# Block-sparse attention and a token/channel mixer on one core: whole k copies, GpSimd casts, and a list that counts changes of partition quarter

## The chip, the cores and the metric

The kernel runs on one core of a Trainium2 chip. A core has five engines that run their own instruction queues and meet at semaphores: TensorE (PE, matmuls and transposes by matmul, results to PSUM), VectorE (DVE), ScalarE (ACT), GpSimd (POOL) and SyncE (SP, which here only issues DMAs). PSUM is the small accumulation memory of PE; SBUF is the working memory, 128 partitions wide. The metric is device time in microseconds of one launch.

## The reference

Four batches, eight heads, 768 positions, head width 64, all in float32. First a block-sparse causal attention, per batch and head:

```python
k_rep = k.reshape(B, H, n_blocks, block, D).mean(axis=3)      # 12 blocks of 64 keys
gate_scores = np.einsum('bhsd,bhnd->bhsn', q, k_rep)           # blocks of the future: -1e9
top_idx = np.argsort(gate_scores, axis=-1)[..., -3:]           # three blocks, and the own one
scores = where(chosen block and key <= query, q @ k.T / 8, -1e9)
attn_out = softmax(scores) @ v
```

The result, heads side by side (512 wide), is x of a mixer: `h = relu(x.T @ w_tok1) @ w_tok2` over positions (768 to 256 to 768), `u = x + h.T`, then `out = u + relu(u @ w_ch1) @ w_ch2` over channels (512 to 1536 to 512).

## The kernel before, in words

The work is cut into 16 **pairs** of heads, four to a batch (`pair(p)`), and one channel MLP for each batch (`mlp(b)`). A pair goes through these steps:

- Load k and q (SP's queue, L491 or L484) and v (GpSimd's queue, L501). In early pairs the loads are plain and PE turns k and q (L424, 128x128 float32 transposes into PSUM buffers called pm). From pair 6 (q) and 7 (k) the loads are so laid out that DVE's 32x32 transposes (L515, L562) do it.
- Sum k over blocks of 64 (DVE, L528 or L517), spread the sums of the two heads to a block-diagonal tile (GpSimd, `spread`, L510), and copy k, cast to float16, into KA, one head after the other (L320 is the copy of DVE and GpSimd, L318 that of ACT). For early k these are four copies of 64 partitions out of PSUM: two halves of 384 positions, two heads.
- Copy q out of PSUM into QT (128 x 384) and cast it head by head into QA.
- The gate: q times block sums (PE, L604; from pair 6 on in three bfloat16 parts, L619), add the causal bias (L608, L624), the third largest of each row (`MAX8`, L635), compare (L648), clear the own block (L655). The resulting mask is turned (PE, L675, or DVE, L660, from pair 5 on) and copied to twelve extra rows of QA; KA has indicator rows there, so that the score matmul adds a large negative number for blocks not chosen.
- Scores (PE, L696, into two PSUM tiles sc of 1024 columns), exp (ACT, L709, into E), causal mask of the diagonal (GpSimd, L717), times v with a column of ones (PE, L726), divide (DVE, L729, L733) into x.
- Token mixer (PE L744, L758; DVE L761 gives u), then u is turned for the channel MLP: by six PE transposes (L772) and a copy (`uT`), or, for the pairs between the leads `ua` and `ub`, by `turned`: DVE block transposes (L430), a store to a scratch tensor in memory (`turn`, L434) and four loads back (L438).

A batch's MLP is 24 groups of four matmuls (L791), a relu each (ACT L799 or DVE L801), and for each of six rows of 128 positions twelve matmuls (L813), the addition of u (L817) and a store (L821).

Pair 0 (`CUT = 1`) is treated in halves so that it can start early: its k, q, gate and mask come in two parts, and its first score tile needs only the first part.

**What sets the order.** Every step is entered in a `Plan` with the engines it may run on, a cost for each, and a priority: the pair's due time `T(p)` less a lead out of the table `L` (in units of the planner). `Plan.run` is a list scheduler: it simulates the engines, takes for the engine that can start first the ready step of the lowest priority, and picks PSUM and SBUF buffers from rings. The instructions are then written out in that order, engine by engine, each engine's queue running in order. Where PE has nothing to do in the planned order, `fill` (L859) puts in matmuls of zeros to an unused PSUM corner, so that PE's clock does not fall. When the last score tile is done, the four halves of the two sc tiles join the ring of the pm buffers.

Lines that the prediction names: L859 zeros; L424 transposes of k and q; L528 k sums; L510 spread; L604 gate; L675 mask transposes; L696 scores; L772 u transposes; L813 last matmuls; L817 addition of u.

Of the kernel before, what the change touches and what calls it, by code (L numbers as in the profile page):

```python
# [52 lines left out]
L = dict(kd=28.39, qd=28.38, vd=14.55, kt=13.31, kr=28.77, ke=-6.18, qt=21.02, qe=-10.99, q16=13.75, g=20.5, b=21.41,  # L53
         k16=21.8, r=25.24, w1=3.91, w2=-6.05, wc1=11.98, wc2=29.44, tok=8.67, ml=11.38, o0=-3.16, o1=2.55, o2=3.04,
         o3=-0.47, o4=-4.49, o5=0.44, o6=-3.74, o7=-7.56, o8=-2.66, o9=-2.98, o10=-2.08, o11=-1.85, o12=5.6,
         o13=-0.18, o14=1.35, o15=1.65, m0=-2.42, m1=5.05, m2=7.96, m3=-1.6, th=5.48, bd=4.61, cu=-9.01, cs=2.59,
         ua=7.09, ub=19.4, ku=23.14, k0=4.38, k1=1.97, qu=19.48, dq=5.5, dk=6.11, va=-12.77)


FREE = {"PE": 800.0, "ACT": 800.0, "DVE": 2200.0, "POOL": 3800.0, "SP": 800.0}  # L60
# [19 lines left out]
class Op:  # L80
    __slots__ = ("n", "cost", "fn", "pr", "deps", "outs", "bufs", "after", "start", "end", "eng", "wait", "not_before", "port", "base", "open")


class Plan:
# [6 lines left out]
    DMA = 1.15  # L91
# [5 lines left out]
    def op(self, cost, fn, rd=(), wr=(), pr=0.0, not_before=0.0, port=False):  # L97
        o = Op()
        o.n, o.cost, o.fn, o.pr, o.not_before, o.port = len(self.ops), cost, fn, pr, not_before, port
# [23 lines left out]
    def run(self, on_slot_end=None, fill=None):  # L123
# [5 lines left out]
        def slot_for(b):  # L129
            r = b.ring  # L130
            i = min(range(len(r.avail)), key=lambda j: r.avail[j])
            return i, r.avail[i]

        shared = [FREE["POOL"]]

# [3 lines left out]
        def start(o, e):  # L139
            t = max(free[e], o.not_before)  # L140
# [27 lines left out]
        while ready:  # L168
# [6 lines left out]
            for e in free:  # L175
# [3 lines left out]
                for o in ready:  # L179
                    c = o.cost.get(e)  # L180
                    if c is None:
                        continue
                    t = start(o, e)
                    if len(c) > 2 and o.pr > -50.0:
                        t = max(t, dma_free - self.AHEAD)
                        if o.pr > -50.0 and any(x[1:] < (o.pr, o.n) and x[0] <= t for x in loads):
# [19 lines left out]
            if e == "PE" and fill:  # L206
                f = fill(o, free[e], t)
                if f:
                    f.n, f.eng, f.start, f.end = -1, e, free[e], t
                    fillers.append(f)  # L210
            free[e] = t + occ
# [10 lines left out]
            for b in o.bufs:  # L222
                if b.ring is None:
                    continue
                if b.slot is None:
                    b.slot, _ = slot_for(b)
# [49 lines left out]
def kernel(  # L276
# [50 lines left out]
    k16r = sring(3, [128, S], F16, "k16")  # L327
# [30 lines left out]
    pidx, nidx, jidx = np.arange(128), np.arange(NB), np.arange(NJ)  # L358
    mrow = 2 * jidx[None, :, None] + (pidx[:, None, None] >= 64)
    gb1 = -1.0e6 * np.maximum(0, nidx[None, None, :] - mrow)  # L360
    both = np.concatenate([gb1, gb1], axis=2)[:, 1:].astype(np.float32)
# [5 lines left out]
    cst = sb(list(both.shape), FP, "cst")  # L367
    cstc = nc.inline_tensor(both, name="cstc").ap()
    gbias = cst
# [4 lines left out]
    nc.gpsimd.affine_select(out=id32, in_=id32, pattern=[[-1, 128]], compare_op=ALU.not_equal, fill=1.0, base=0, channel_multiplier=1)  # L374
    ks2 = [sb([128, 2, NB], FP, f"ks2_{i}") for i in range(2)]
# [50 lines left out]
    def turned(src, dst, rd, wr, pr, c):  # L426

        tp, d = Buf(k16r), Buf(turnr)
        for i in range(2):
            P.op({"DVE": (487.0, 570.0)}, lambda i=i: nc.vector.transpose(  # L430
                out=tp.t.rearrange("p (f g t) -> p g f t", f=4, t=32)[:, 3 * i:3 * i + 3], in_=src()[:, halves(i)].rearrange("p (g f t) -> p g f t", f=4, t=32)),
                 rd=rd[i], wr=[(tp, i)], pr=pr)
# [16 lines left out]
    def split(src, dst, part, rd, kp, pr):  # L449
# [8 lines left out]
        P.op({"POOL": (850.0, 930.0)}, steps, rd=rd, wr=[(src, 2), (kp, 0), (kp, 1)], pr=pr)  # L458

    def pair(p):  # L460
# [5 lines left out]
        cut = p < CUT  # L466
        straight_q, straight_k = p >= L["dq"], p >= L["dk"]
# [13 lines left out]
        for t, src, e, lead in ((k32, ks_, "SP", "kd"), (q32, qs, "ACT" if p == 0 else "SP", "qd")):  # L481
            if straight_k if t is k32 else straight_q:
                for f in range(4):
                    P.op({e: (570.0, 1600.0, 768 * 13.0 / 16)}, lambda f=f, t=t, src=src, e=e: ENG[e].dma_start(  # L484
                        out=t.t.rearrange("p j x d -> p (j x d)")[32 * f:32 * f + 32].rearrange("t (g i) -> t g i", i=32),
                        in_=src[f // 2, :, 32 * (f % 2):32 * (f % 2) + 32].rearrange("(g t) i -> t g i", t=32)), wr=[(t, f)], pr=t0 - L[lead])
                continue
            for x in range(2):
                for i in range(1 + cut):
                    n = NJ // (1 + cut)  # L490
                    P.op({e: (570.0, 1600.0, 128 * n * 17.6 / 16)}, lambda x=x, t=t, src=src, e=e, i=i, n=n: ENG[e].dma_start(  # L491
                        out=t.t[:, n * i:n * i + n, x, :], in_=src[x, 128 * n * i:128 * n * i + 128 * n].rearrange("(j p) d -> p j d", p=128)),
                        wr=[(t, (x, i) if cut else x)], pr=t0 - L[lead] - (99.0 - 0.2 * i if p == 0 else 0.0))
        if p == 0:
            P.op({"ACT": (1500.0, 1600.0)}, lambda: nc.scalar.activation(out=warm, in_=zero[:, 0:1], func=AF.Exp), pr=-98.0)
            P.op({"ACT": (450.0, 1600.0, 128 * 45 / 16)}, lambda: nc.scalar.dma_start(out=cst, in_=cstc), wr=[(fixed, "cst")], pr=-99.0)
        if p < 3:
            e = "SP" if p else "ACT"
            P.op({e: (450.0, 1600.0, 24 * 135 / 16)}, lambda e=e: ENG[e].dma_start(out=KA.t[64:KR], in_=indc), wr=[(KA, "ind")],
                 pr=t0 - L["qd"] + 0.2 if p else -98.9)  # L500
        P.op({"POOL": (1100.0, 2200.0, 1536 * 17.6 / 16)}, lambda: nc.gpsimd.dma_start(  # L501
            out=VA.t[:, :, :, 0:64], in_=vs.rearrange("x (j p) d -> p x j d", p=128)), wr=[(VA, 0)], pr=t0 - L["vd"])
# [5 lines left out]
        def spread(z):  # L508
            for x in range(2):
                nc.gpsimd.tensor_copy(out=ks2b.t[64 * x:64 * x + 64, x, z], in_=ks3.t[64 * x:64 * x + 64, 0, z])  # L510

        if straight_k:
            KT = Buf(KTr)
            for i in range(2):
                P.op({"DVE": (487.0, 570.0)}, lambda i=i: nc.vector.transpose(  # L515
                    out=KT.t[:, halves(i)], in_=k32.t.rearrange("p j x d -> p (j x d)")[:, halves(i)]), rd=loaded(k32, i), wr=[(KT, i)], pr=t0 - L["ku"])
            P.op({"DVE": (862.0, 945.0)}, lambda: nc.vector.tensor_reduce(  # L517
                out=ks3.t[:, 0], in_=KT.t.rearrange("c (n w) -> c n w", w=64), axis=AX.X, op=ALU.add), rd=[(KT, 0), (KT, 1)], wr=[(ks3, 0), (ks3, 1)], pr=t0 - L["kr"])
            for x in range(2):
                P.op({"POOL": (772.0, 820.0), "ACT": (721.0, 825.0), "DVE": (470.0, 555.0)}, lambda e, x=x: copy(ENG[e], KA.t[0:64, x, :], KT.t[64 * x:64 * x + 64]),  # L520
                     port=True, rd=[(KT, 0), (KT, 1)], wr=[(KA, (x, 0)), (KA, (x, 1))], pr=t0 - L["ke"])
            if not thirds:
                P.op({"POOL": (380.0, 450.0)}, lambda: spread(slice(0, NB)), rd=[(ks3, 0), (ks3, 1)], wr=[(ks2b, 0), (ks2b, 1)], pr=t0 - L["kr"] + 0.1)
        else:
            for i in range(2):
                t = Buf(Rr)
                P.op(pe(slow=3), lambda t=t, i=i: transposed(k32, i, t.t), rd=loaded(k32, i), wr=[(t, 0)], pr=at(i, L["kt"]))
                P.op(dve(HS), lambda t=t, i=i: nc.vector.tensor_reduce(  # L528
                    out=ks3.t[:, 0, 6 * i:6 * i + 6], in_=t.t[:, 0:HS].rearrange("c (n w) -> c n w", w=64),
                    axis=AX.X, op=ALU.add), rd=[(t, 0)], wr=[(ks3, i)], pr=at(i, L["kr"]))  # L530
                if not thirds and (cut or i == 1):
                    z = slice(6 * i, 6 * i + 6) if cut else slice(0, NB)
                    P.op({"POOL": (380.0, 450.0)}, lambda z=z: spread(z), rd=[(ks3, i)] if cut else [(ks3, 0), (ks3, 1)],
                         wr=[(ks2b, i)] if cut else [(ks2b, 0), (ks2b, 1)], pr=at(i, L["kr"]) + 0.1)
                if dual:
                    continue
                for x in range(2):
                    def kev(e, t=t, i=i, x=x):
                        copy(ENG[e], KA.t[0:64, x, halves(i)], t.t[64 * x:64 * x + 64, 0:HS])
                    P.op({**dve(HS), **act(HS)}, kev, rd=[(t, 0)], wr=[(KA, (x, i))], pr=at(i, L["ke"]))  # L540
        if thirds:
            split(ks3, lambda x: kp.t[64 * x:64 * x + 64, :, x, :], lambda h, x: h[64 * x:64 * x + 64], [(ks3, 0), (ks3, 1)], kp, t0 - L["kr"] + 0.1)
        if dual:
            k16 = Buf(k16r, "k16")
            P.op({"POOL": (778.0, 828.0)}, lambda: nc.gpsimd.tensor_copy(
                out=k16.t.rearrange("p (j c) -> p j c", c=128), in_=k32.t.rearrange("p j x d -> p j (x d)")), rd=loaded(k32, 0), wr=[(k16, 0)], pr=t0 - L["k16"])
# [356 lines left out]
```

## Time and profile before

| what | us |
|---|---|
| median of 3 runs | 251.23 (250.78 to 254.77) |
| the profiled execution itself | 251.01 |
| its span, first to last instruction | 249.3 |
| PE busy in the span | 241.2 |
| DVE / ACT / POOL busy | 168.0 / 167.3 / 119.9 |

The page gives busy time by engine, then groups of instructions by source line. The timeline has rows of start, duration, engine, line, operation, tiles (out<-in) and count; in brackets stands the idle time of that engine just before, and what ended it. "PEld" is the weight load of a matmul, "SPq" or "ACTq" a queue that issues DMAs. The answer by stretches gives for each stretch of the span the busy time of each engine, the granted clock of PE and the share of time that the DMA engines are busy (over 1 when packets of several queues are in flight on one engine). The granted clock is 1.00 in all stretches that the prediction uses.

### The profile page before, as it was taken

The page shows a single profiled execution, that of the slowest core. Times are in us where ns is not written, and L with a number is a line of the kernel's source. Part 1 is how long each engine was busy: PE and PEld are TensorE (multiplying, and loading weights), DVE is VectorE, ACT ScalarE, POOL GpSimd, SP SyncE. Part 2 cuts the span into 40 slices and gives each one's busy share as a digit, 9 for nine tenths or more (in the row PEclk, how much of TensorE's full clock was granted, in tenths as well). Part 3 has the DMA queues.
Part 4 walks back from the last instruction along what each step waited for, and adds up shares of the span by engine and source line. Part 5 has one row for each costly group of instructions (what it writes and reads, how often), then busy time and mean ns, then how long its engine had stood idle before and what let it go on. Part 6 is the DMA issues. An engine that isn't in the chain of part 4 may idle for free.

```text
span 249.3 us, 6629 instructions
## 1 busy us (share of the span) xinstructions
PE 241.2 (97%) x2478; PEld 164.8 (66%) x2478; DVE 168.0 (67%) x538; ACT 167.3 (67%) x259; POOL 119.9 (48%) x264
## 2 busy tenths in 40 slices
PE   8899899999999999999999999999999999999994
PEld 8788587887656676667665766567756665554643
DVE  4699988988618889999998899799344522112112
ACT  2487979998768597978997688279744662340620
POOL 5065777568438586787788648453111110000000
PEclk9999999999999999999999999999999999999999
DMA  8999999999829899989899983320221211112112
GB/s 147 218 194 189 207 165 170 170 150 111 141 28 168 152 162 153 130 145 184 146 113 154 190 152 63 106 86 5 67 89 63 74 29 45 42 42 87 43 42 84
DMA packets 119816, 29.31 MB, mean 118 GB/s; under 512 B 113348, under 2 KB 116292, under 8 KB 119784
## 3 DMA queue, kind: packets, MB, share of 16 engines
q1 hardware_dynamic: 89952, 21.32, 42.7%
q0 software_dynamic: 28064, 7.08, 30.2%
q10 hardware_dynamic: 1768, 0.49, 0.9%
q8 instruction: 19, 0.31, 0.6%
q14 instruction: 13, 0.11, 0.2%
HBM read 28.29 MB, written 7.67 MB: 144 GB/s over the span
## 4 chain that ended last, share of the span: by engine, by line
PE 78%; DVE 9%; SPq 4%; issue 3%; POOL 2%; ACT 2%; DMA 2%; DVEq 0%; POOLq 0%
PE pm L791 18%; PE pm L813 17%; PE sc L696 11%; PE pm L726 7%; PE sc L813 4%; SPq L484 4%; PE sc L791 3%; PE pm L744 3%; PE pm L758 3%; PE pm L424 3%; PE pm L604 2%; PE pm L859 2%; DMA q<-in_q_dram 2%; PE pm L619 1%; DVE KA L320 1%
## 5 line engine op out<-in xcount | busy, mean ns | idle before, releaser
L709 ACT ACTIVATE E<-sc 128x1024 f16<-128x1024 f32 (+2 forms) x96 | 84.3, 915 | 22.4 <-PE sc L696 20.9
L717 POOL TENSOR_SCALAR_AFFINE_SELECT E<-E 128x256 f16<-128x256 f16 (+1 forms) x96 | 39.4, 416 | 52.4 <-ACT E L709 50.1
L791 PE MATMUL pm<-uT,wc 128*128 128x384 f16 x332 | 62.0, 326 | 0.0
L813 PE MATMUL pm<-wc,h 128*128 128x512 f16 x240 | 58.2, 379 | 0.0
L791 PEld LDWEIGHTS <-wc 128*128 128x128 f16 x384 | 35.8, 98 | 22.5 <-issue 0.2
L696 PE MATMUL sc<-QA,KA 76*128 76x512 f16 (+3 forms) x264 | 48.4, 301 | 0.3
L813 PEld LDWEIGHTS <-h 128*128 128x128 f16 x312 | 28.4, 98 | 26.4 <-issue 0.7
L799 ACT ACTIVATE h<-pm 128x384 f16<-128x384 f32 x62 | 30.2, 491 | 12.7 <-PE pm L791 12.6
L696 PEld LDWEIGHTS <-KA 76*128 76x128 f16 x264 | 23.5, 98 | 14.3 <-issue 0.8
L817 DVE TENSOR_TENSOR os<-u,pm 128x512 f32<-128x512 f16 x20 | 13.6, 681 | 26.9 <-PE pm L813 25.1
L726 PEld LDWEIGHTS <-E 128*128 128x128 f16 x672 | 25.3, 98 | 4.3 <-issue 0.7
L726 PE MATMUL pm<-VA,E 128*128 128x65 f16 x651 | 26.0, 193 | 0.6 <-DVE QT L320 0.5
L318 ACT CAST QA<-QT 64x768 f16<-64x768 f32 (+1 forms) x23 | 18.4, 801 | 2.5 <-DVE QT L562 2.0
L733 DVE TENSOR_TENSOR x<-pm,rc 128x384 f16<-128x384 f32 x31 | 17.2, 554 | 0.8
L799 ACT ACTIVATE h<-sc 128x384 f16<-128x384 f32 x13 | 6.2, 490 | 16.4 <-DVE os L817 8.7
L761 DVE TENSOR_TENSOR u<-x,pm 128x384 f16<-128x384 f16 x31 | 15.9, 545 | 1.8 <-PE pm L758 1.6
L501 POOL DMA_DIRECT2D VA<-in_v_dram x16 | 16.9, 1056 | 0.4 <-issue 0.2
L801 DVE TENSOR_SCALAR h<-pm 128x384 f16<-128x384 f32 x21 | 11.3, 548 | 6.8 <-PE pm L791 3.7
L729 DVE RECIPROCAL rc<-pm 128x6 f32<-128x6 f32 x31 | 5.8, 187 | 12.5 <-PE pm L726 12.3
L744 PEld LDWEIGHTS <-w 128*128 128x128 f16 x192 | 12.0, 98 | 2.5 <-issue 0.7
L758 PEld LDWEIGHTS <-w 128*128 128x128 f16 x192 | 12.0, 98 | 2.3 <-issue 0.5
L635 DVE MAX8 m<-gm 128x8 f32<-128x12 f32 x160 | 13.0, 156 | 0.3
(85 smaller groups left out, 342.7 us busy)
## 6 DMA issues: line engine op xcount, KB each, us to landing
out_dram<-os SPq DMA_DIRECT2D x23, 256.0 KB, 2.2
k<-in_k_dram SPq DMA_DIRECT2D x40, 96.0 KB, 3.3
q<-in_q_dram SPq DMA_DIRECT2D x40, 96.0 KB, 2.7
VA<-in_v_dram POOLq DMA_DIRECT2D x16, 192.0 KB, 5.8
wc<-in_moe_w_ch_dram POOLq DMA_DIRECT2D x8, 384.0 KB, 5.4
k<-in_k_dram SPq DMA_DIRECT2D x12, 192.0 KB, 5.3
q<-in_q_dram SPq DMA_DIRECT2D x10, 192.0 KB, 5.6
turn<-k SPq DMA_DIRECT2D x7, 192.0 KB, 3.6
```

Of the source, the lines that this page charges most:

```text
L318: e.copy(out=out, in_=in_)
L501: P.op({"POOL": (1100.0, 2200.0, 1536 * 17.6 / 16)}, lambda: nc.gpsimd.dma_start(out=VA.t[:, :, :, 0:64], in_=vs.rearrange("x (j p) d -> p ...
L696: nc.tensor.matmul(out=s.t[:, at:at + 128 * m], lhsT=KA.t[:, x, 128 * kk:128 * kk + 128], rhs=QA.t[:, q0:q0 + m, x, :], start=True, stop=True)
L709: nc.scalar.activation(out=E.t[:, BASE[g_]:BASE[g_ + 1]], in_=s.t[:, 0:WIDTH[g_]], func=AF.Exp, scale=scale)
L717: nc.gpsimd.affine_select(out=o, in_=o, pattern=[[0, len(d)], [1, 128]], compare_op=ALU.is_ge, fill=0.0, base=0, channel_multiplier=-1)
L726: nc.tensor.matmul(out=t[:, jq, :], lhsT=E.t[:, cc:cc + 128], rhs=VA.t[:, x, kk, :], start=(kk == 0), stop=(kk == jq))
L733: P.op(dve(384), lambda a=a, rc=rc, x=x: nc.vector.tensor_tensor(out=xp.t[:, :, 64 * x:64 * x + 64], in0=a.t[:, 0:NJ * 65].rearrange("p (j ...
L744: nc.tensor.matmul(out=m1.t[:, 128 * t:128 * t + 128], lhsT=w1[:, j, 128 * t:128 * t + 128], rhs=xp.t[:, j, :], start=(j == 0), stop=(j == ...
L758: nc.tensor.matmul(out=m.t[:, 128 * j:128 * j + 128], lhsT=w2[:, t, 128 * (j0 + j):128 * (j0 + j) + 128], rhs=h1.t[:, t, :], start=(t == 0 ...
L791: nc.tensor.matmul(out=m.t[:, 0:HS], lhsT=wc1[:, c, 128 * f:128 * f + 128], rhs=uT.t[:, c].rearrange("p (a w) -> p a w", a=4)[:, :, 96 * i ...
L799: nc.scalar.activation(out=o, in_=w, func=AF.Relu)
L813: nc.tensor.matmul(out=m.t[:, 0:wide], lhsT=h2.t[:, f, 128 * jj:128 * jj + 128], rhs=wc2[:, f, w:w + wide], start=(f == 0), stop=(f == NFC ...
```

## The change

1. **k of early pairs.** For pairs 1 to 6 the two PSUM halves of k are each copied whole, 128 partitions by 384, to a float16 tile k16 in SBUF (ACT or DVE). From there GpSimd or DVE copies each head (64 x 768) into KA. Pair 0 keeps its copies out of PSUM, now behind the k sum.
2. **q casts** of pairs 1 to 5 are given to GpSimd alone (lead `qp`); the `spread` of block sums may go to DVE.
3. **The list** counts changes of partition quarter: each step says from which memory and quarter it reads and to which it writes (`io`), and a step whose quarter differs from the one before on its engine starts later by `HELD`. It also prefers, among free PSUM buffers, pm over halves of sc; costs of DMAs are set lower (`DMA` 1.1, v's packets 16.0), and a load waits for others that are due within 900 ns.
4. **The first gate and the loads.** k and q of pair 0 are split over SP's and ACT's queues head by head (before: k on SP, q on ACT). The causal bias is made by GpSimd in place of a load. Early pairs have a table of leads of their own (`e...`), and all leads have new values; `ua` 7.09 becomes 3.23 (pairs 4 to 14 are `turned`, before 8 to 14), `bd` 4.61 becomes 5.16 (from pair 6 on DVE turns the mask).
5. One store of the last batch is cut in three, so that the number of DMAs is a multiple of eight.

As issued, the program has 103 matmuls of zeros in place of 95, 30 u transposes in place of 54, 30 mask transposes in place of 25; 12 whole k copies, 12 casts from k16 (7 on GpSimd, 5 on DVE); q's casts 15 on GpSimd (before 8), 13 on ACT (before 21) and 2 on DVE (before 1); 12 of 14 spread copies on DVE.

```diff
-FREE = {"PE": 800.0, "ACT": 800.0, "DVE": 2200.0, "POOL": 3800.0, "SP": 800.0}
+LEADS = ("kd", "qd", "vd", "kt", "kr", "ke", "qt", "qe", "q16", "g", "b", "tok")
+FREE = {"PE": 800.0, "ACT": 800.0, "DVE": 2200.0, "POOL": 3300.0, "SP": 800.0}
...
-    DMA = 1.15
+    DMA = 1.1
+    HELD = {"DVE": 115.0, "ACT": 130.0, "POOL": 85.0}
...
+            twin = lambda j: r.avail[j ^ 1] if r.name == "R" and j >= 4 else 0.0
+            return min(range(len(r.avail)), key=lambda j: (max(r.avail[j], t - self.SYNC), twin(j), r.avail[j]))
...
+        def held(o, e):
+            if not o.io or e not in places or len(o.cost[e]) > 2:
+                return 0.0
+            src, dst = o.io[0].split(">")
+            at = places[e]
+            marks = ["r" + src[i:i + 2] for i in range(0, len(src), 2)] + ["w" + dst]
+            return self.HELD[e] if any(at.get(m[:2], m[2]) != m[2] for m in marks) else 0.0
...
         def start(o, e):
-            t = max(free[e], o.not_before)
+            t = max(free[e] + held(o, e), o.not_before)
...
-    cst = sb(list(both.shape), FP, "cst")
-    cstc = nc.inline_tensor(both, name="cstc").ap()
+    gbias = sb([128, NJ - 1, 2 * NB], FP, "gbias")
+    nc.gpsimd.memset(gbias, 0.0)
+    nc.gpsimd.affine_select(out=o, in_=o, pattern=[[128, NJ - 1], [0, 2], [-64, NB]], compare_op=ALU.is_ge, fill=-1.0e6, base=128, channel_multiplier=1)
...
+        lead = {n: L["e" + n if p < PPB else n] for n in LEADS}
...
             for x in range(2):
+                e = "ACT" if p == 0 and x else "SP"
...
+                if not cut:
+                    def kout(e, t=t, i=i):
+                        copy(ENG[e], k16.t[:, halves(i)], t.t[:, 0:HS])
+                    P.op({**dve(HS), **act(HS)}, kout, rd=[(t, 0)], wr=[(k16, i)], io="P0>S0", pr=at(i, lead["ke"]))
                     continue
...
+        if not straight_k and not dual and not cut:
+            for x in range(2):
+                P.op({"POOL": (772.0, 820.0), "DVE": (300.0, 380.0)}, lambda e, x=x: copy(ENG[e], KA.t[0:64, x, :], k16.t[64 * x:64 * x + 64]),
+                     port=True, rd=[(k16, 0), (k16, 1)], wr=[(KA, (x, 0)), (KA, (x, 1))], io=f"S{2 * x}>S0", pr=t0 - lead["ke"] + 0.1)
...
-                P.op({"POOL": (772.0, 820.0), "ACT": (721.0, 825.0), "DVE": (470.0, 555.0)} if not cut else {"DVE": (300.0, 380.0), "ACT": (410.0, 510.0)},
-                     q16, port=True, ...
+                P.op({"DVE": (300.0, 380.0), "ACT": (410.0, 510.0)} if cut else {"POOL": (772.0, 820.0)} if p < L["qp"] else
+                     {"POOL": (772.0, 820.0), "ACT": (721.0, 825.0), "DVE": (470.0, 555.0)}, q16, port=True, ...
```

More of the change, by code (lines that the diff above doesn't have):

```diff
@@ L80 @@
 class Op:
-    __slots__ = ("n", "cost", "fn", "pr", "deps", "outs", "bufs", "after", "start", "end", "eng", "wait", "not_before", "port", "base", "open")
+    __slots__ = ("n", "cost", "fn", "pr", "deps", "outs", "bufs", "after", "start", "end", "eng", "wait", "not_before", "port", "base", "open", "io")
 class Plan:
@@ L185, in run @@
                         t = max(t, dma_free - self.AHEAD)
-                        if o.pr > -50.0 and any(x[1:] < (o.pr, o.n) and x[0] <= t for x in loads):
+                        if o.pr > -50.0 and any(x[1:] < (o.pr, o.n) and x[0] <= t + 900.0 for x in loads):
                             continue
@@ L783, in mlp @@
         n = 0
+        even = -sum(1 for o in P.ops for e, x in o.cost.items() if len(x) > 2 and e != "POOL") % 8 if b == B - 1 else 0
         for i in range(2):
```

163 lines of the change are left out of this document (88 added, 75 removed).

## The prediction

> **What bounds the kernel now.** First the page's head and the busy time by stretch: where is TensorE (PE) not full?
>
> ```profile
> span 249.3 us, 6629 instructions
> ...
> PE 241.2 (97%) x2478; PEld 164.8 (66%) x2478; DVE 168.0 (67%) x538; ACT 167.3 (67%) x259; POOL 119.9 (48%) x264
> ```
>
> ```profile
> core 0: us, PE busy (x) PEld busy (x) DVE busy (x) ACT busy (x) POOL busy (x), PEclk, DMA share, GB/s
> 0.00:13.57 13.57, 11.04 (x111) 10.18 (x112) 7.75 (x31) 5.36 (x11) 4.94 (x26) 1.00 1.13 184
> 13.57:20.00 6.43, 5.81 (x57) 5.02 (x57) 6.13 (x22) 5.57 (x9) 3.73 (x9) 1.00 1.42 196
> 20.00:30.00 10.00, 9.45 (x110) 7.37 (x110) 9.55 (x31) 8.52 (x12) 6.69 (x18) 1.00 1.17 199
> 30.00:40.00 10.00, 9.65 (x131) 7.87 (x128) 8.41 (x39) 8.68 (x12) 6.66 (x17) 1.00 1.57 159
> 40.00:100.00 60.00, 59.85 (x733) 43.54 (x732) 47.49 (x152) 49.22 (x77) 40.39 (x84) 1.00 1.07 140
> 100.00:150.00 50.00, 49.92 (x536) 32.79 (x534) 46.83 (x148) 42.10 (x63) 37.76 (x72) 1.00 1.03 152
> ```
>
> From 40 us on PE is full, so what leaves PE there is worth its whole time and what any other engine saves is worth nothing by itself. Before 40 us PE idles 2.53 us up to its first scores at 13.57 and 0.62 + 0.55 + 0.35 = 1.52 us behind them; much of the rest of the front is L859, matmuls of zeros that compute nothing. So the timeline of the front is read next.
>
> ```profile
> 0.82 2.13 ACTq L491 DMA_DIRECT2D q<-in_q_dram  x4
> ...
> 0.82 4.01 SPq L491 DMA_DIRECT2D k<-in_k_dram  x6
> ...
> 1.07 3.33 PEld L859 LDWEIGHTS <-zero 128*128 128x128 f16 x34 [1.07 <-DVE zero L372]
> ...
> 1.09 0.29 POOL L374 TENSOR_SCALAR_AFFINE_SELECT id<-id 128x128 f32<-128x128 f32 x1
> ...
> 4.45 0.85 PE L424 MATMUL pm<-id,k 128*128 128x128 f32 x3
> ...
> 5.09 0.85 PE L424 MATMUL pm<-id,q 128*128 128x128 f32 x3
> 5.34 0.56 DVE L528 TENSOR_REDUCE ks<-pm 128x6 f32<-128x384 f32 x1 [2.54 <-PE pm L424]
> ...
> 5.81 1.11 DVE L320 CAST KA<-pm 64x384 f16<-64x384 f32 x2
> ...
> 5.98 0.48 ACT L318 COPY QT<-pm 128x384 f32<-128x384 f32 x1 [1.50 <-PE pm L424]
> ...
> 6.60 0.78 PE L604 MATMUL pm<-ks,QT 128*128 128x12 f32 x4
> 6.96 0.55 DVE L320 CAST QA<-QT 64x384 f16<-64x384 f32 x1
> ...
> 7.82 1.15 PEld L859 LDWEIGHTS <-zero 128*128 128x128 f16 x20
> ...
> 9.19 0.54 DVE L528 TENSOR_REDUCE ks<-pm 128x6 f32<-128x384 f32 x1
> ...
> 10.24 0.85 PE L604 MATMUL pm<-ks,QT 128*128 128x24 f32 x6 [1.11 <-POOL ks L510]
> ...
> 11.40 0.82 DVE L635 MAX8 m<-gm 128x8 f32<-128x12 f32 x10
> ...
> 12.14 0.30 DVE L648 TENSOR_TENSOR bn<-pm,m 128x72 f16<-128x72 f32 x2
> ...
> 12.43 0.19 DVE L655 MEMSET bn<- 64x6 f16 x2
> ...
> 13.06 0.96 ACT L318 COPY QA<-pm 12x384 f16<-12x384 f16 x2
> ...
> 13.57 0.93 PE L696 MATMUL sc<-QA,KA 76*128 76x256 f16 x9
> ...
> 15.14 1.02 DVE L320 COPY QT<-pm 128x384 f32<-128x384 f32 x2
> ...
> 16.20 0.55 DVE L320 CAST QA<-QT 64x768 f16<-64x768 f32 x1
> 16.30 1.13 POOL L320 CAST QA<-QT 64x768 f16<-64x768 f32 x1 [0.42 <-DVE QT L320]
> ```
>
> The chain to the first scores: k transposed, k summed (DVE), sums spread (POOL), gate (PE), top three and mask (DVE), mask transposed (PE) and copied (ACT). Its worst hole is before the second gate at 10.24: the second k sum starts only at 9.19, behind DVE's two k casts and the q copies.
>
> **Term 1, the front: -2.9 us.** The order of the changed kernel walked with the durations above:
> - 28 zeros in place of 34, at 3.33/34 = 0.098 us: PE is free at 1.07 + 2.7 = 3.8. The first k halves now head both load queues.
>
> ```profile
> DMA to landing us min/median/max: 2.6/3.6/6.2
> ```
>
> - At the least of this row (k, first 8 us) they land at 0.82 + 2.6 = 3.4, so the zeros still decide. k transposes 3.8; four zeros; q transposes 4.8.
> - Sum 0.89 behind its transposes (5.34 against 4.45): 4.7 to 5.3. The spread is DVE's now: no such DVE row; between the memset pair (0.19) and a pair of half-height casts (1.11), nearest the memset by size, I take 0.3: 5.6. q's copy 0.89 behind its transposes, on DVE: 5.7 to 6.25. First gate about 6.4 (was 6.60).
> - DVE goes on with q's cast (to 6.8), the second k sum (to 7.35, was 9.73), the first half of the gate scores (0.15), the spread (to 7.8), four MAX8 (0.33), compare and memset: half of the mask at about 8.5 (was 12.62).
> - ACT has k casts, QA cast, k cast, then the second q copy, to 8.35: second gate 8.4 (was 10.24), to 9.25.
> - Two mask transposes and the next pair's six k transposes (1.2 us) on PE, while ACT finishes two casts and copies the half mask (under 0.96): first scores at 10.5.
>
> That is 3.1 earlier, less 0.2 for three mask transposes that move behind. Bounds: -1.5 (the whole mask is needed by the second scores anyway and lands on the same DVE) to -4.0 (spread at 0.19, nothing queued at ACT).
>
> **Term 2, new zeros behind the first scores: +2.5 us.** The order has 60 zeros after the first scores, 17 before the change: the list sees holes there (16, 10 and 11 in a row between the scores of pairs 1 to 2). 43 x 1.15/20 = 2.5. Bounds +1.0 (they stand where PE would have idled, 1.52 now) and +3.2 (each of some six more holes is longer than its zeros by two pitches). The front's gain thus partly runs into ACT and DVE, which cannot follow at that speed.
>
> **Term 3, waits behind the first scores: -1.0 us.**
>
> ```profile
> PEld pm L424 <- DVE KA L320: 1.7, 3, 0.8
> ```
>
> The transposes of k and q wait for PSUM buffers that DVE's half-height k casts hold. Now a buffer is read by the sum and one whole copy (0.51 each in the pair at 15.14) instead of the sum and two casts (0.555 each). Also the list now charges VectorE, ScalarE and GpSimd for a change of partition quarter; the two pairs of rows, 1.02 and 1.11, show that such a charge exists, so waits that the order did not foresee should shrink. Of 1.52 I take 1.0; bounds 0 and -1.5.
>
> **Term 4, PE work: -1.06 us.** Lead "ua" goes from 7.09 to 3.23: u of pairs 4 to 7 is turned by DMA, 24 transposes fewer; "bd" keeps pair 5's mask on PE, five more.
>
> ```profile
> 44.74 0.67 PE pm L744 x12
> ```
>
> 128 columns take 0.67/12 = 0.056: 19 fewer are -1.06, all where PE is full.
>
> **Term 5, the end: -0.4 us.**
>
> ```profile
> 245.63 0.49 PE L813 MATMUL sc<-wc,h 128*128 128x128 f16 x6 [0.38 <-DVE os L817]
> ```
>
> The last two output sums lie in halves of one sc tile; the second waits until DVE has read the first. Now they lie in two pm tiles, and the late MLP uses no sc half at all: four buffers in place of eight. Its cover: a relu takes 0.49, a group of PE 0.65.
>
> ```profile
> L799 ACT ACTIVATE h<-pm 128x384 f16<-128x384 f32 x62 | 30.2, 491 | 12.7 <-PE pm L791 12.6
> ```
>
> A fourth-last buffer has three groups' time, 1.95, to be read. If that cover went, each group would wait some tenths.
>
> **Costed at nothing:** the bias made by GpSimd (two instructions more, at most 0.29 each by the row at 1.09; the loads hide them, and without that cover the first V load starts 0.6 later, long before E needs V); KA's indicator rows, now ACT's fifth load issue in place of its sixth, as the constant's is gone; one out store of the last batch cut in three, two more issues for SP while PE computes the last batch.
>
> Sum: -2.9 + 2.5 - 1.0 - 1.06 - 0.4 = -2.9. The profiled run took 251.01 us (span 249.3 and 1.7 around it; median of the runs 251.23): **248.1 us**, own range 246.2 to 250.5.
>
> **Rivals.**
>
> *GpSimd is the next late one.* It takes on 7 k casts and 7 q casts net, most before 60 us.
>
> ```profile
> L320 POOL CAST KA<-KT 64x768 f16<-64x768 f32 x10 | 8.2, 818 | 2.6 <-DVE bn L648 1.3 <-DVE KT L515 1.1
> ...
> L320 POOL COPY QA<-bnt 12x384 f16<-12x384 f16 x16 | 8.0, 499 | 4.9 <-DVE bnt L660 4.4
> ```
>
> At 0.82 (fp16 input is not shown; half the columns take 0.50) that is 11.5 us. The masks of E queue behind them. The cast at 16.30 took 1.13 while DVE's cast at 16.20 ran: 0.31 more. If all 14 meet DVE so and PE waits each time: 14 x 0.31 = 4.3, 252.4 us. For it: DVE is 9.55 of 10 busy from 20 to 30. Against: POOL has 3.3 us free in each 10. It decides once POOL is past 9.5 of 10 there. [...]
>
> *Slower: the loads.*
>
> ```profile
> q1 hardware_dynamic: 89952, 21.32, 42.7%
> ```
>
> ```profile
> SPq L434 <- DVE k L430: 17.5, 4, 5.8
> ```
>
> The DMA share is above 1 from 40 to 150 us. A packet of q1 takes 0.427 x 249.3 x 16/89952 = 0.019 us on one engine; a turned u is 1024 packets, 1.2 us of all 16; four more are 4.8 us, between 60 and 100. SP also issues in order: pair 8's k and q now stand behind turn stores, which wait for DVE up to 5.8 us. PE would stand at the gates of pairs 8 to 12, which it meets in order. If the loads lag by the whole 4.8 and the front's gain is eaten there: 251.0 - 1.06 - 0.4 + 4.8 = 254.3 us. Against: the gates of pairs 9 to 15 stand later in PE's order than before (pair 15's now behind pair 14's scores). It decides when a gate's k lands after PE has reached it.
>
> *More than forecast.* Front -4.0, zeros +1.0 (they cover what were waits), waits -1.5, then -1.06 and -0.5: -6.1, 244.9 us. For it: the list now knows costs that the trace shows.
>
> **How the numbers follow.** Forecast 0.46, GpSimd 0.20 (250 to 253), loads 0.12 (252.8 to 257), more 0.22 (243.5 to 246.2). The range 244.6 to 252.8 leaves out the loads and the lowest of the last. Two per cent, about what a measurement of this kernel tells from no change, is 5.0 us: below 246.2 lies the last case and an edge of the first, 0.24; above 256.3 a part of the loads, 0.05; within 0.71.
>
> **What would show it.** Term 1: first scores near 10.5 us, second gate near 8.4. Term 2: zeros of 0.5 us and more between 15 and 35 us, with ACT at 9 tenths. Term 3: no wait of k transposes on DVE casts. Term 4: 30 u transposes. Term 5: no wait of the last sums on DVE. GpSimd: casts over 1 us, E masks late and PE waiting on them. Loads: PE idle at the gate line between 85 and 140 us. I am wrong if PE is no longer full behind 40 us.

## The result, and the profile after

The changed kernel took 247.43 us (median of 6 runs, 246.32 to 251.24); the kernel before, on the same chip, 251.14 (median of 6). The ratio is 0.985, 95% interval 0.981 to 0.988: 3.7 us less by the medians, forecast 3.1 (251.2 to 248.1). The profiled execution is the lowest of the six, 246.32 with a span of 244.6, so 4.7 below the profiled one of before. Ratios and their intervals, here and below, leave out runs that lie over 1.5% above the kernel's lowest; medians keep them.

The page's head, and the answer by stretches:

```profile
span 244.6 us, 6642 instructions
...
PE 238.1 (97%) x2467; PEld 162.9 (67%) x2467; DVE 170.4 (70%) x546; ACT 160.6 (66%) x251; POOL 128.2 (52%) x263
```

```profile
0.00:10.61 10.61, 8.01 (x74) 7.23 (x75) 5.74 (x30) 5.50 (x11) 3.75 (x21) 1.00 1.14 175
10.61:20.00 9.39, 8.41 (x110) 7.14 (x108) 8.13 (x30) 7.98 (x13) 7.35 (x15) 1.00 1.33 207
20.00:30.00 10.00, 10.00 (x121) 8.75 (x117) 8.66 (x34) 7.71 (x11) 7.58 (x13) 1.00 1.34 211
30.00:40.00 10.00, 9.91 (x142) 7.85 (x141) 8.33 (x38) 7.68 (x11) 8.63 (x19) 1.00 1.95 168
40.00:100.00 60.00, 59.99 (x720) 43.18 (x719) 51.79 (x153) 44.41 (x72) 42.08 (x85) 1.00 1.01 148
100.00:150.00 50.00, 50.00 (x541) 33.16 (x540) 46.05 (x142) 40.93 (x61) 38.29 (x75) 1.00 1.19 167
```

But for 0.1 us PE is busy from 20 us on, where it was from 40. Busy is not the same as useful, though: 39 of the matmuls between 20 and 30 us are zeros, some 2 us of time, and between 20 and 40 us 216 matmuls that compute start, where it was 220. The lead is made before: by 20 us 128 of them have started, where it was 88. ACT went down from 167.3 to 160.6, GpSimd up from 119.9 to 128.2. The timeline of the front, with the rows that answer to those of before:

```profile
3.85 0.85 PE L446 MATMUL pm<-id,k 128*128 128x128 f32 x3
...
4.74 0.56 DVE L553 TENSOR_REDUCE ks<-pm 128x6 f32<-128x384 f32 x1 [2.94 <-PE pm L446]
...
5.41 0.34 DVE L534 COPY ks<-ks 64x6 f32<-64x6 f32 x2
5.78 0.56 DVE L344 COPY QT<-pm 128x384 f32<-128x384 f32 x1
...
6.49 0.58 PE L639 MATMUL pm<-ks,QT 128*128 128x12 f32 x4 [0.15 <-DVE QT L344]
...
6.85 0.54 DVE L553 TENSOR_REDUCE ks<-pm 128x6 f32<-128x384 f32 x1
...
8.53 0.82 PE L639 MATMUL pm<-ks,QT 128*128 128x24 f32 x6 [0.71 <-DVE bn L683]
...
10.61 0.83 PE L731 MATMUL sc<-QA,KA 76*128 76x256 f16 x10
...
22.82 1.00 PE L899 MATMUL pm<-zero 128*128 128x120 f16 x16
```

The whole list of PE's waits:

```profile
PE pm L899 <- DVE zero L391: 1.1, 1, 1.1
PE pm L639 <- DVE bn L683: 0.7, 1, 0.7
PE pm L446 <- DMA k<-in_k_dram: 0.7, 2, 0.3
PE pm L446 <- DMA q<-in_q_dram: 0.6, 1, 0.6
PE sc L731 <- DVE QA L344: 0.3, 1, 0.3
PE pm L639 <- DVE QT L344: 0.2, 1, 0.2
```

All of them lie before 15 us. Three are for loads (0.7 for k, 0.6 for q, all but the first for the pairs behind pair 0), a wait that PE's list of before does not have. The waits of the k transposes on DVE's casts and that of the last sums on DVE are gone.

### The profile page after: what moved, and what is told of

It is laid out like the page before. It is cut to its first block, busy times and chain, and to the rows that moved or that the text cites. A ratio compares the mean times of both kernels' runs of the same rounds, so it can differ in the third digit from the quotient of the medians.

```text
span 244.6 us, 6642 instructions
## 1 busy us (share of the span) xinstructions
PE 238.1 (97%) x2467; PEld 162.9 (67%) x2467; DVE 170.4 (70%) x546; ACT 160.6 (66%) x251; POOL 128.2 (52%) x263
## 4 chain that ended last, share of the span: by engine, by line
PE 91%; DMA 3%; DVE 3%; issue 0%; SPq 0%; POOL 0%; POOLq 0%
PE pm L827 26%; PE pm L849 25%; PE sc L731 14%; PE pm L761 9%; PE pm L779 4%; PE pm L793 4%; DMA k<-in_k_dram 3%; PE pm L639 2%; PE pm L654 2%; PE pm L446 2%; PE pm L710 1%; PE pm L899 1%; DVE ks L553 1%; DVE ks L534 1%; PE pm L807 1%; DVE m L670 1%
## 5 line engine op out<-in xcount | busy, mean ns | idle before, releaser
L827 PE MATMUL pm<-uT,wc 128*128 128x384 f16 x384 | 69.9, 326 | 0.0
L849 PE MATMUL pm<-wc,h 128*128 128x512 f16 (+2 forms) x312 | 68.8, 363 | 0.0
L835 ACT ACTIVATE h<-pm 128x384 f16<-128x384 f32 x71 | 34.5, 491 | 28.2 <-PE pm L827 28.0
L853 DVE TENSOR_TENSOR os<-u,pm 128x512 f32<-128x512 f16 (+2 forms) x26 | 16.6, 640 | 33.9 <-PE pm L849 33.2
L796 DVE TENSOR_TENSOR u<-x,pm 128x384 f16<-128x384 f16 x32 | 16.5, 542 | 4.7 <-PE pm L793 4.7
L837 DVE TENSOR_SCALAR h<-pm 128x384 f16<-128x384 f32 x25 | 13.8, 554 | 8.5 <-PE pm L827 7.5
L768 DVE TENSOR_TENSOR x<-pm,rc 128x384 f16<-128x384 f32 x32 | 17.8, 555 | 0.9
L793 PE MATMUL pm<-h,w 128*128 128x128 f16 x192 | 13.8, 219 | 0.0
L342 ACT COPY QA<-bnt 12x384 f16<-12x384 f16 x20 | 10.2, 508 | 5.3 <-DVE bnt L695 4.9
L779 PE MATMUL pm<-x,w 128*128 128x128 f16 x192 | 13.3, 219 | 0.0
```

The source lines that it names most:

```text
L768: P.op(dve(384), lambda a=a, rc=rc, x=x: nc.vector.tensor_tensor(out=xp.t[:, :, 64 * x:64 * x + 64], in0=a.t[:, 0:NJ * 65].rearrange("p (j ...
L779: nc.tensor.matmul(out=m1.t[:, 128 * t:128 * t + 128], lhsT=w1[:, j, 128 * t:128 * t + 128], rhs=xp.t[:, j, :], start=(j == 0), stop=(j == ...
L793: nc.tensor.matmul(out=m.t[:, 128 * j:128 * j + 128], lhsT=w2[:, t, 128 * (j0 + j):128 * (j0 + j) + 128], rhs=h1.t[:, t, :], start=(t == 0 ...
L827: nc.tensor.matmul(out=m.t[:, 0:HS], lhsT=wc1[:, c, 128 * f:128 * f + 128], rhs=uT.t[:, c].rearrange("p (a w) -> p a w", a=4)[:, :, 96 * i ...
L835: nc.scalar.activation(out=o, in_=w, func=AF.Relu)
L849: nc.tensor.matmul(out=m.t[:, 0:wide], lhsT=h2.t[:, f, 128 * jj:128 * jj + 128], rhs=wc2[:, f, w:w + wide], start=(f == 0), stop=(f == NFC ...
```

## The experiments

Each kernel was timed against the kernel before. In the table the last column has those runs in which PE's granted clock stood at 0.998 or more over the whole run; why it is needed is told at zeros_gone. Below, these runs are compared with each other, and medians with medians. zeros_gone, k_in_place and closer_zeros keep the changed kernel's order of work; by the traces turn_undone keeps PE's up to 62 us and slots_undone up to 200. The others are planned anew from the front on, and what that alone can cost is seen at jitter_a.

| kernel | median us | ratio to before, 95% | runs at full clock, us |
|---|---|---|---|
| changed kernel | 247.43 | 0.985 (0.981 to 0.988) | 246.32, 246.54 |
| front_only | 254.09 | 1.011 (1.010 to 1.013) | 253.28, 253.30 |
| turn_undone | 248.28 | 0.988 (0.986 to 0.990) | 247.28 |
| slots_undone | 247.10 | 0.984 (0.981 to 0.986) | 245.90 |
| zeros_gone | 250.60 | 0.984 (0.982 to 0.986), from 3 of its 12 runs | 246.17, 247.60 |
| old_leads | 250.61 | 1.001 (0.998 to 1.003) | 249.68 to 250.48 |
| k_undone | 251.12 | 1.001 (0.998 to 1.004) | 249.15, 249.63 |
| q_undone | 250.76 | 0.997 (0.994 to 1.001) | 249.00 to 249.81 |
| quarters_undone | 251.93 | 1.002 (0.999 to 1.004) | 249.65 |
| jitter_a | 255.47 | 1.020 (1.016 to 1.023) | none |
| jitter_b | 250.78 | 0.998 (0.995 to 1.001) | 248.82, 248.91 |
| k_in_place | 249.30 | 0.995 (0.992 to 0.998) | 248.76 to 249.21 |
| closer_zeros | 246.81 | 0.984 (0.981 to 0.986) | 246.13 to 246.98 |

**front_only: the front alone, on the kernel before.**

```diff
-        for t, src, e, lead in ((k32, ks_, "SP", "kd"), (q32, qs, "ACT" if p == 0 else "SP", "qd")):
+        for t, src, e, lead in ((k32, ks_, "SP", "kd"), (q32, qs, "SP", "qd")):
             for x in range(2):
+                e = "ACT" if p == 0 and x else "SP"
...
-                nc.gpsimd.tensor_copy(out=ks2b.t[64 * x:64 * x + 64, x, z], in_=ks3.t[64 * x:64 * x + 64, 0, z])
+                ENG[e].tensor_copy(out=ks2b.t[64 * x:64 * x + 64, x, z], in_=ks3.t[64 * x:64 * x + 64, 0, z])
```

(with the bias by GpSimd and the new leads of pair 0)

> The kernel before with the front alone changed: pair 0's loads split over SP and ACT by head, the bias made by GpSimd, its spread open to DVE, its leads those of the change. Theory (the early start carries through, because PE is full behind it): first scores about 3 us earlier than the 13.57 of before, and of that at least half reaches the end, 248.5 to 249.8 us. Rival (the front runs into ScalarE and VectorE, which set the pace from 14 to 40 us, and the gain is only real together with the relief of those two): first scores early too, but PE idle and zeros between 14 and 40 us grow by as much, and the time stays within 0.7 us of before.

The first scores start at 11.34, 2.2 earlier than before, and the kernel is 3.2 us slower than before by the medians. By stretches:

```profile
20.00:30.00 10.00, 9.65 (x94) 7.41 (x91) 9.26 (x31) 9.19 (x15) 4.84 (x12) 1.00 1.16 207
30.00:40.00 10.00, 9.97 (x140) 8.63 (x139) 8.29 (x38) 8.58 (x13) 6.19 (x17) 1.00 1.75 178
40.00:50.00 10.00, 8.80 (x120) 6.89 (x117) 7.32 (x28) 8.65 (x13) 6.32 (x13) 1.00 1.34 162
```

DVE and ACT are over 9 of 10 busy from 20 to 30 while GpSimd is at 4.84; PE idles 1.2 between 40 and 50. Behind the first scores stand 58 matmuls of zeros where 17 stood before: 41 more, at 0.052 us each 2.1 us, as much as the early start gained, while PE's idle time from the first scores to 60 us stays as it was (1.64 and 1.67). So far the rival is right: the early start runs into zeros, and the two engines that empty PSUM are the ones that are nearly full. Why the kernel is 3 us slower on top of that isn't shown; it has a new order too, and the profiled run has one stretch at half clock (10.7 to 14.1 us).

**turn_undone, slots_undone: `ua` back to 7.09; the old choice of a PSUM buffer.**

```diff
-          ua=3.23, ...
+          ua=7.09, ...
```

```diff
-            return min(range(len(r.avail)), key=lambda j: (max(r.avail[j], t - self.SYNC), twin(j), r.avail[j]))
+            return min(range(len(r.avail)), key=lambda j: r.avail[j])
```

> The changed kernel with lead ua back at 7.09: u of pairs 4 to 7 is turned by PE again, 24 transposes of 0.056 us. Theory (PE is full behind 40 us): 1.3 us slower than the changed kernel, 247.7 us for a profiled run against 246.3. Rival (the four stores and sixteen loads more cost DMA time that PE waits for at the gates): no slower, or up to 1 us faster, and less PE idle between 85 and 120 us.

> The changed kernel with PSUM buffers picked as before, the longest free first, halves of sc included. Theory (a wait on the other half of one sc tile cost time at the end): PE waits again behind 200 us, 0.4 to 1.2 us in all, and the run is that much slower than the changed kernel. Rival (four pm buffers instead of eight cost as much in waits on the relus as they save): no difference beyond 0.3 us.

turn_undone has 54 u transposes again and takes 0.85 us more by the medians, 0.74 to 0.96 at full clock (one run): the theory's sign, at two thirds of its 1.3. slots_undone is no slower (its rival is right), and in its trace too PE has no hole over 0.1 us behind 200 us: that rule alone isn't what removed the wait of the last sums. turn_undone's price comes near to one in a held order, but it is no surer than the half microsecond by which slots_undone lies below the changed kernel at full clock.

**zeros_gone: no zeros behind a planned 10 us.**

```diff
-        if mlp_on or n < 2:
+        if mlp_on or n < 2 or a > 10000.0:
```

> The changed kernel without the 60 matmuls of zeros that stand behind its first scores; everything else is in the same order, and the result is the same. Theory (the zeros stand where PE would idle, as holes of the order): no faster than 0.4 us, and the idle time of PE between 11 and 57 us grows by about 2 to 3 us, as much as the zeros took. Rival (the zeros are themselves a cost, run before work that is ready): 1.5 to 3 us faster. A third way: slower by 0.5 us or more, if matmuls run slower after idle time.

The third way came, by the clock of PE: two runs of twelve are at full clock, ten take 249.60 to 252.96. Stretches of 3.4 us of a profiled run (the column before the last two is the granted clock):

```profile
4.70:8.10 3.40, 2.77 (x29) 2.20 (x27) 3.03 (x12) 2.02 (x5) 0.00 (x0) 1.00 1.56 185
8.10:11.50 3.40, 2.26 (x22) 2.09 (x23) 2.46 (x17) 2.31 (x6) 0.00 (x0) 1.00 1.35 225
11.50:15.00 3.50, 3.31 (x18) 1.95 (x17) 3.36 (x8) 2.42 (x5) 2.26 (x6) 0.51 1.21 214
15.00:18.40 3.40, 3.40 (x18) 3.17 (x17) 0.33 (x2) 1.83 (x2) 2.97 (x5) 0.50 0.85 184
18.40:21.80 3.40, 3.40 (x32) 2.71 (x30) 2.52 (x17) 2.52 (x4) 1.24 (x3) 0.50 1.21 177
21.80:25.00 3.20, 3.20 (x50) 2.94 (x48) 2.48 (x6) 1.13 (x3) 2.61 (x4) 1.00 0.91 195
```

PE idles 1.14 of the 3.40 us up to 11.5, no hole longer than 0.71; then the clock stands at half for three stretches. At full clock the two runs, 246.17 and 247.60, stand beside 246.32 and 246.54: no gain is shown, and a loss of up to 1 us isn't excluded. That fits zeros that stand where PE would idle. What they buy is the clock: without them it falls in ten of twelve runs, for three or four stretches by the mean clock (0.972 to 0.979); with them in four of six.

The changed kernel itself has this in smaller measure. Its six runs by mean clock: 246.32 (1.000), 246.54 (0.999), 247.31 and 247.54 (0.993), 248.09 (0.986), 251.24 (0.973). Each 0.007 is one stretch of 3.4 us at half clock (3.4/2/245), so there were one, one, two and four, and costs 0.8 to 1.2 us.

**old_leads: the whole code of the change with the leads of before.**

```diff
-L = dict(kd=28.39, qd=24.29, vd=11.04, ... etok=17.72)
+L = dict(kd=28.39, qd=28.38, vd=14.55, ... (the values of before, for early pairs too), qp=5.5)
```

> The changed kernel with the due times of before: every lead in the table, early pairs too, has the value it had (so u of pairs 4 to 7 is turned by PE again and pair 5's mask by DVE); whole k copies, GpSimd casts, counted quarters, the new loads and the bias stay. Theory (the parts themselves carry the gain, the table only fits them): 247.5 to 249.5 us. Rival (an early start and freed engines are worth little until the due times of the steps behind them are moved to use it; the front alone was 3.2 us slower than before): 250.5 us or more, with PE idle and zeros between 14 and 50 us above the 6.8 us of the changed kernel.

By the medians no gain is left (250.6), at full clock some 0.5 us (249.68 to 250.48, where before took 250.4 to 251.7 beside it): the rival is right in the main. The reverse, a table fitted anew to the code of before, wasn't tried; so how much of the gain the search for a better table would give without the parts stays open.

**k_undone, q_undone, quarters_undone: one part undone, all leads new.**

```diff
-                if not cut:
+                if False:
                     def kout(e, t=t, i=i):
```

```diff
-          ... dq=5.5, qp=5.5, ...
+          ... dq=5.5, qp=0.5, ...
```

```diff
-    HELD = {"DVE": 115.0, "ACT": 130.0, "POOL": 85.0}
+    HELD = {"DVE": 0.0, "ACT": 0.0, "POOL": 0.0}
```

> The changed kernel, but k of pairs 1 to 6 copied again head by head out of PSUM, four copies to a pair, on VectorE or ScalarE. Theory (PSUM buffers held by these copies made PE wait, and VectorE and ScalarE set the pace of the front): 0.8 to 2.5 us slower than the changed kernel, with waits of the k and q transposes on copies back in the trace. [...]

> The changed kernel, but q's casts of pairs 1 to 5 may go to any of GpSimd, ScalarE and VectorE again. Theory (ScalarE's exps set the pace from 14 to 40 us and casts stand in their way): 0.3 to 1.5 us slower. Rival (GpSimd late, casts meeting VectorE's copies): as fast or up to 1 us faster, since the list may pick the freest engine.

> The changed kernel with the list's charges for a change of partition quarter set to zero. Theory (a list that knows these waits puts its zeros and steps where the chip has them): 0.5 to 2 us slower, with more PE idle and fewer zeros (92 for 103) between 10 and 40 us. Rival (an order like any other): within 0.4 us.

Each alone loses nearly the whole gain, 2.5 to 3.5 us at full clock and 3.3 to 4.5 by the medians: three parts with all of it each cannot be a sum. Either each is needed, or any disturbance of the planned order costs this much. Two tests tell these apart.

**jitter_a, jitter_b: nothing undone, every lead moved at random by up to 0.3 us (but those that switch a pair from one way to another, such as ua).**

```diff
-L = dict(kd=28.39, qd=24.29, vd=11.04, kt=13.4, ke=-12.17, ...)
+L = dict(kd=28.17, qd=24.5, vd=11.2, kt=13.25, ke=-12.2, ...)
```

> The changed kernel with every lead of the table moved at random by up to 0.3 us (a pair takes 16.5), and nothing else: all parts of the change are kept. Each part undone alone took the time back to 250.6 to 251.9, nearly the whole gain. Theory 'the table fits one order': it is the particular order that the table gives that is worth 3 to 4 us, and any disturbance of the list loses it; then this kernel too takes 249.5 to 251.5 us, and what a part undone alone costs is mostly that. Rival 'the parts carry it': the order is not so sensitive, this kernel stays within 1.2 us of the changed one (246.3 to 248.6), and k's whole copies, q's casts and the quarter charge are each worth about 3 us in this order.

> The same with another draw of the random moves. Theory 'the table fits one order': 249.5 to 251.5 us. Rival 'the parts carry it': 246.3 to 248.6. If the two draws differ by more than 1.5 us from each other, the order itself is worth that much, and the cost of a part undone alone cannot be read as the price of the part.

With every part in place the time is 255.5 and 250.8; jitter_b at full clock 248.82 and 248.91, 2.3 to 2.6 above the changed kernel, and jitter_a has no run at full clock. By stretches, jitter_a and then jitter_b:

```profile
10.00:20.00 10.00, 9.91 (x54) 8.50 (x55) 4.57 (x23) 5.37 (x9) 5.23 (x10) 0.50 1.29 211
...
100.00:150.00 50.00, 48.84 (x523) 31.86 (x520) 45.86 (x140) 38.69 (x59) 38.86 (x77) 1.00 1.08 163
```

```profile
10.00:20.00 10.00, 9.87 (x85) 8.48 (x86) 5.73 (x27) 7.02 (x12) 5.89 (x11) 0.69 1.12 193
...
100.00:150.00 50.00, 48.43 (x507) 31.32 (x504) 43.62 (x127) 39.88 (x57) 36.84 (x71) 1.00 1.20 165
```

Both lose in two places: the granted clock is 0.50 and 0.69 between 10 and 20 us, and PE idles again after 100 us (1.2 and 1.6), where the changed kernel is full. The theory that the table fits one order holds; so the price of an undone part cannot be read from the three kernels above, nor from old_leads and front_only. The fall of the clock isn't the leads' doing alone, as the changed kernel has it in four of six runs; the 2.3 to 2.6 us at full clock are the measure.

**k_in_place: k's copies undone, the order held.**

```diff
-                        copy(ENG[e], k16.t[:, halves(i)], t.t[:, 0:HS])
+                        for x in range(2):
+                            copy(ENG[e], KA.t[0:64, x, halves(i)], t.t[64 * x:64 * x + 64, 0:HS])
...
-lambda e, x=x: copy(ENG[e], KA.t[0:64, x, :], k16.t[64 * x:64 * x + 64]),
+lambda e, x=x: None,
```

> The changed kernel with its order of work held: the planner plans whole copies of k as in the changed kernel, but at the place of each whole copy (pairs 1 to 6, twelve copies of 128x384) two half-height casts straight into KA are made by the same engine, and the later copies into KA (which GpSimd mostly did) are not made at all. PE, ACT and DVE keep the order and the places of the changed kernel; only the engines' times differ: about 0.6 us more in each of twelve places on DVE or ACT (1.11 a pair for 0.51 one), 7 us between 10 and 85 us, and some 8 us less on GpSimd. When k's copies were undone with a new plan the time was 251.1, 3.7 above the changed kernel. Theory 'the order is what was lost': here the loss is at most 1.2 us, 247.0 to 248.6. Rival 'the whole copy itself carries the gain': the PSUM buffers are held 0.6 us longer each time, PE waits behind most of the twelve, 249.5 to 252.

The median falls between the two forecasts. Six of its twelve runs are at full clock, 248.76 to 249.21, 2.2 to 2.9 above the changed kernel. Its timeline near 22 us, and then that of the changed kernel at the same place:

```profile
22.34 1.95 ACT L342 CAST KA<-pm 64x384 f16<-64x384 f32 x4 [2.00 <-PE pm L446]
...
25.39 0.43 PE L732 MATMUL sc<-QA,KA 76*128 76x512 f16 x2 [1.04 <-ACT E L745]
```

```profile
21.82 0.86 ACT L342 CAST k<-pm 128x384 f16<-128x384 f32 x2 [2.17 <-PE pm L446]
...
22.59 2.54 ACT L744 ACTIVATE E<-sc 128x1024 f16<-128x1024 f32 x3
```

The casts hold ACT 1.95 in place of 0.86, the exps start later, and the scores wait 1.04 for a PSUM tile. PE is busy 8.39 and 8.77 of 10 between 10 and 30 us, against 9.02 and 10.00. With the order held, k's whole copies are worth about 2.5 us in this order, which was fitted to them. Sixteen of the 24 casts are ACT's here and the longest new wait names its exps, so the place is at least in part ACT's. That is no step back to the kernel before, which had 20 of its 28 half-height casts (pair 0's included) on DVE. How much q's casts and the quarter charge carry in a held order wasn't tried.

**closer_zeros: zeros priced by what they take.**

```diff
-        n = int((b - max(a, at + 60.0)) / (54.0 if a > 16000.0 else 104.0) - 1.0)
-        if mlp_on or n < 2:
+        n = int((b - max(a, at + 60.0)) / (54.0 if a > 7000.0 else 104.0) - 1.0)
+        if mlp_on or n < 1:
```

> The changed kernel with the planner's zeros priced 54 ns in place of 104 from the planned 7 us on, and single zeros allowed: holes between 7 and 16 us are filled about twice as densely (14, 1, 8, 5, 6 zeros where 7, 0, 3, 2, 2 stood; 124 in all for 121). Theory: the dips of the granted clock that cost the changed kernel 0.8 to 1 us each come from holes of TensorE between 5 and 14 us; with them filled most runs show a clock of 1.0, and the median falls from 247.4 to 246.3 (0.3 to 1.1 less than the changed kernel). Rival 'zeros only get in the way': each new zero lies before work that was ready, the front grows by up to 17 x 0.055 = 0.9 us and the clock dips as often: 247.4 to 248.3.

Median 246.81, and all six runs lie between 246.13 and 247.65: one of six has a half-clock stretch where the changed kernel had four. At full clock it gains nothing. Its interval overlaps that of the changed kernel, so a gain of 0.6 in the median isn't proven, and six runs are few to call the missing tail shown.

## Why the prediction was right

Forecast -2.9 against the profiled run, measured -4.7 (its clock at 1.00 throughout, and the lowest of its six runs) and -3.7 by the medians. The main case came, with every sign right, and the front came nearly step by step. The sizes are less sure than the total: by the busy time of the views the five terms add up to -3.2 and 0.3 lies behind the last matmul; the other 1.2 lies in time that the records call busy, where the ends of matmuls are modelled, and no term named it. That the median comes so near is in part luck: the profiled runs, both at full clock, gained 1.8 more than forecast, and the clock took back 1.0 of it in the median.

- **Term 1, the front.** First scores forecast at 10.5, seen at 10.61 (-2.96; the term's -2.9 has 0.2 off for mask transposes that move behind). Step by step, forecast and seen: k transposes 3.8 / 3.85; q 4.8 / 4.76; first gate 6.4 / 6.49; second k sum 6.8 / 6.85; second gate 8.4 / 8.53. The spread on DVE, taken at 0.3 between bounds of 0.19 and 1.11, took 0.34.
- **Term 2, zeros.** +2.5 forecast, +2.2 in the trace: behind the first scores stand 17 zeros before and 60 after, at 0.052 each (the row at 22.82: 16 in 1.00, the last of them 0.22 long), 0.9 and 3.1. As a row of the sum it stands; as the price of zeros it was wrong in kind: zeros_gone gains nothing at full clock without them. Terms 2 and 3 are better read as one: PE's time behind the first scores that computes nothing, zeros and idle time to 200 us, rose from 0.9 + 1.75 to 3.1 + 1.08, by 1.5, as the two terms together said. So about half of what the front gained was lost behind it.
- **Term 3, waits.** -1.0 forecast; by the busy time of the views PE's idle time from the first scores to 200 us falls from 1.75 to 1.08, -0.7. Counted between the starts of matmuls, beyond the pitch of their shape, it falls by 1.0 to 2.0, an estimate that depends on the pitch taken. The transposes' wait on DVE's casts is gone as forecast. Whether the gain came from DVE, where the step looked for it, isn't settled; k_in_place shows that ACT's share in the copies counts too.
- **Term 4, PE work.** -1.06 forecast, as 24 u transposes fewer (-1.34) and five mask transposes more (+0.28). turn_undone puts the 24 back and costs 0.85, in an order that is the same up to 62 us: the sign is shown, the size only roughly. The mask transposes were priced too low, 0.056 each: five of them take 0.47 in the row at 24.81 of the changed kernel. 30 u transposes, as forecast:

```profile
L807 PE MATMUL pm<-id,u 128*128 128x128 f16 x30 | 2.5, 219 | 0.0
```

- **Term 5, the end.** -0.4 forecast, -0.7 measured in idle time behind 200 us. By stretches, before and then after, each nearly to PE's last matmul:

```profile
200.00:245.60 45.60, 44.95 (x296) 25.35 (x295) 9.10 (x16) 15.92 (x34) 1.22 (x3) 1.00 0.13 49
```

```profile
200.00:241.30 41.30, 41.30 (x273) 23.36 (x270) 7.73 (x14) 13.85 (x29) 0.00 (x0) 1.00 0.14 50
```

  After idles nothing there; before had, beside the hole of the last sums (0.38), one of 0.30 at 204.9 that the forecast did not name:

```profile
205.20 0.83 PE L744 MATMUL sc<-x,w 128*128 128x128 f16 x12 [0.30 <-DVE x L733]
```

  Which edit closed them isn't settled: neither the slot rule nor the leads alone, since slots_undone and old_leads lack them too.
- **GpSimd as the next late one** didn't come. It is 7.58 and 8.63 of 10 busy from 20 to 40 us, short of the 9.5 that the forecast named, and no wait in PE's list names it. Its meetings with DVE are there, in the timeline of the changed kernel:

```profile
11.79 0.82 POOL L344 COPY KA<-k 64x768 f16<-64x768 f16 x1 [0.19 <-DVE k L344]
...
12.14 1.44 DVE L534 COPY ks<-ks 64x12 f32<-64x12 f32 x2
...
13.50 0.72 DVE L344 COPY QA<-pm 12x384 f16<-12x384 f16 x2
...
13.89 0.98 PE L731 MATMUL sc<-QA,KA 76*128 76x384 f16 x7 [0.32 <-DVE QA L344]
...
14.05 0.81 POOL L344 CAST QA<-QT 64x768 f16<-64x768 f32 x1 [0.49 <-ACT QT L342]
14.25 0.82 DVE L344 COPY KA<-k 64x768 f16<-64x768 f16 x1
...
18.10 0.48 DVE L534 COPY ks<-ks 64x12 f32<-64x12 f32 x2
...
24.48 0.35 DVE L344 COPY KA<-k 64x768 f16<-64x768 f16 x1
```

  A KA copy of DVE takes 0.82 where it starts behind a cast of GpSimd (at 14.25, the cast at 14.05) and 0.35 where it starts first (at 24.48); the two copies of a spread take 1.44 where GpSimd's KA copy and masks of E run, and 0.48 where only the first of them meets the end of a KA copy. The copy at 14.25 ends at 15.07, 0.21 behind GpSimd's cast; what holds it isn't shown. The loss falls mostly on DVE: its five KA copies take 0.35 to 0.87, GpSimd's seven KA copies and 15 q casts 0.81 to 0.84. Once PE pays: the copies of the mask start only behind the spread of 1.44, and the scores at 13.89 wait 0.32 for them.
- **Slower, the loads** didn't come: the stores of turned u wait up to 10.1 us for DVE, 9.6 where the wait is for the turning transposes (forecast: up to 5.8),

```profile
SPq L456 <- DVE k L452: 17.8, 5, 9.6
SPq L456 <- DVE rc L764: 14.1, 2, 10.1
```

  and still PE has no wait at a gate behind 15 us.
- **More than forecast** came near in the runs at full clock (246.3 to 246.5; that case began at 246.2), by the time that no term named and by term 5. The prediction had no case in which PE's clock falls below 1.00; that it falls in four of six runs brings the median back by 1.0.

## What to carry to other kernels

Where an order of work has been fitted, undo a part with the order held before you price it: here a random 0.3 us on the leads cost nearly as much as any part, 2.3 to 2.6 us at full clock. Fit the table to the old code anew as well; that wasn't done here, so the gain belongs to the parts and the new table together. An earlier start pays only if what it runs into can follow: alone it turned into zeros (41 more, 2.1 us, in front_only). Count zeros apart from work when PE looks full. And where the clock falls in some runs of one program, compare runs of equal clock before medians.

## What the runs showed of the hardware

The clock of PE fell to half for 3.4 us, or two, three or four times that, in nine of the fourteen traces, always once and between 9 and 12 us while work was under way. It lasted 3.4 us in front_only, turn_undone, slots_undone (0.50 from 10.3 to 13.7 us) and old_leads, and by the mean clock of the stretches about 6.8 in q_undone and jitter_b, 10.2 in zeros_gone and 13.6 in quarters_undone and jitter_a. No hole near it was longer than 0.93 us (quarters_undone). In the 3.4 us before the fall PE was busy 2.0 to 2.7 by the trace (2.26 in zeros_gone). But as much idle time elsewhere left the clock at 1.00, in the kernel before and then in q_undone:

```profile
7.00:10.41 3.41, 2.30 (x31) 2.12 (x31) 2.07 (x4) 1.46 (x4) 0.37 (x2) 1.00 1.39 230
```

```profile
111.60:115.01 3.41, 1.85 (x30) 1.22 (x27) 3.30 (x11) 2.07 (x4) 3.21 (x4) 1.00 1.37 144
```

So neither the longest hole nor the idle share of a stretch, as the trace shows them, decides; what does stays open. And the same order of work falls in one run and not in another: slots_undone, the changed kernel's up to 200 us, falls at 10.3 us in its trace, the changed kernel doesn't (1.00 throughout). Why is not shown. In front_only, turn_undone, slots_undone and old_leads the clock came back after 3.4 us; in zeros_gone it took about 10.2, with PE busy 3.31 of 3.50 and then twice 3.40 of 3.40 by the trace, and in quarters_undone about 13.6.
